# Attention and two expert layers on one core: the second layer's weight decode gets a timetable of its own, and the first layer's last output products alternate with the second layer's first input products

## The chip, the cores and the metric

One NeuronCore of a Trainium2 chip runs the whole program in one launch. The metric is the device time of one execution in microseconds (us). The engines are TensorE (PE, matmuls), VectorE (DVE), ScalarE (ACT), GpSimd (POOL) and the queue of transfers that SyncE issues (SP). Each works through its own instructions in the order of the program and waits on semaphores of the others.

## What is computed

```
q_pool = q.reshape(B, H, S // 2, 2, D).mean(axis=3)           # B 4, H 8, S 1152, D 64
attn   = softmax(q_pool @ k^T / sqrt(D))                      # per head
x      = (attn @ v) as 2304 tokens x 512

h = x @ w_in          # layer 1: 512 -> 2048
g = h * cos(h)
x = g @ w_out         # 2048 -> 512

h = x @ w_in2         # layer 2, with weights of its own
g = h * sigmoid(h)
out = g @ w_out2
```

All inputs arrive as 64-bit numbers, the weights of both layers too.

## The kernel before

**Attention, then layer 1.** The attention ends at 863 us of the span. Its matmuls are mixed with those of layer 1, which works on 9 blocks of 256 tokens (the ninth collects the left-over tokens of the four batches and can only begin after the attention). A block goes through 16 steps f. Step f makes 128 rows of h with 12 matmuls (`g1_unit`, L573): every product is made of three, of float16 high and low parts. Two steps share a PSUM buffer `h`, which ACT copies to `hk` (L589). Each 4 steps make a group G: DVE and ACT form h·cos h (DVE L601, L602, ACT sine L608, DVE L611), DVE casts the high part `gh` (L616) and POOL subtracts to get the low part `gl` (L617). The 12 matmuls of step f towards the block's output y (`g2_unit1`, L628) lag 12 steps behind. A finished y is copied by ACT (L637) to a buffer of the ring `tt` (2 buffers, the same that the cosine groups use) and stored (L640). The generator `layer1` yields after each of these units of 12 matmuls; the caller pulls it with `next(units)`.

**The decode of layer 2's weights** runs beside this. There are 16 pieces, i0 to i7 of `w_in2` and o0 to o7 of `w_out2`. A piece is loaded by SP into one of 3 buffers of the ring `wst`; ACT takes the absolute value (L220), DVE finds the maximum and shifts the bits into place (L221, L224, L229, L232), two small DVE instructions and a PE matmul (`bm`, L97) make the piece's common scale, DVE writes it (L100, L104, L108: `si` or `so`), and ACT and POOL write the float16 parts: for an i piece two ACT passes (L284, L285) and one POOL subtraction `il` (L286); for an o piece one ACT pass (L263), four POOL subtractions of 128x256 (L267), four ACT copies into the operand tables `ops` (L257) and four POOL subtractions (L258, three of 128x512 and one of 128x256). Then the ring's buffer is free, and the next piece is loaded into it.

**Layer 2** computes its h with the same `g1_unit` (its input `ys` is split by ACT L1036 and DVE L1037), and its output by outer products (`outer_steps`, L742) that use seven sums of the weight blocks instead of eight (tables `ops5`, `ops2`). The outer products need all of o0 to o7, and their tiles `op` lie in the memory that the ring `wst` gives back, so they can begin when the last o piece is done.

**What sets the order.** The generator `weight_steps` yields 4 to 5 times per piece. Before, the decode ran one piece ahead of the writing, and it was stepped once for each unit of layer 1 after the attention until the last i piece was written; then all remaining units of layer 1 ran, and the rest of the decode was stepped once for each f of layer 2. It was run to its end after block `TAIL_G - 2` of layer 2, that is after the third block. The final order of the instructions on each engine is then set by a scheduler with priorities (`ahead`, `early`).

Of the kernel before, what the change touches and what calls it, by code (L numbers as in the profile page):

```python
# [11 lines left out]
F32 = mybir.dt.float32  # L12
# [18 lines left out]
W2_BUFS, W2_PACE, W2_N = 3, 6, 1  # L31
# [15 lines left out]
def attention_moe_moe_kernel(ctx, tc, q, k, v, w_in1, w_out1, w_in2, w_out2, out):  # L47
# [32 lines left out]
    def scale_steps(m, pool, res, top, wide=False):  # L80

        n = m.shape[1]
        if wide:
            w = small.tile([128, 1], F32, name="mw", tag="mw")
            wi, mi = w.bitcast(I32), m.bitcast(I32)
            nc.vector.tensor_scalar(
                out=wi, in0=mi, scalar1=3, scalar2=0x3F800000, op0=ALU.logical_shift_left, op1=ALU.bitwise_and  # L90
            )
            nc.vector.scalar_tensor_tensor(
                out=wi, in0=mi, scalar=1 << 30, in1=wi, op0=ALU.bitwise_and, op1=ALU.bitwise_or
            )
            m = w
        bc = pool.tile([128, 2, GW], F32, tag="h", name="bm")[:, 0, 0:4]
        nc.tensor.matmul(bc[:, 0:n], mean, m, start=True, stop=True)  # L97
        yield
        s, u = res
        nc.vector.tensor_scalar(  # L100
            out=u, in0=bc[:, 0:n], scalar1=TINY, scalar2=2.0**(9 - top), op0=ALU.max, op1=ALU.mult
        )

        nc.vector.tensor_scalar(  # L104
            out=s.bitcast(I32), in0=u.bitcast(I32), scalar1=EXP_MASK, scalar2=EXP_MASK,
            op0=ALU.bitwise_and, op1=ALU.bitwise_xor,
        )
        nc.vector.tensor_scalar(  # L108
            out=u.bitcast(I32), in0=u.bitcast(I32), scalar1=EXP_MASK, scalar2=None, op0=ALU.bitwise_and
        )  # L110
# [46 lines left out]
    def weight_steps(w, srcs, stage, pspool, eng, nsub, bufs, ahead, wt_bufs=WT_BUFS):  # L157
# [16 lines left out]
        def more():  # L174
            if todo:
                kind, p, h = todo.pop(0)
                c, n = shape(kind)
                dt = I32 if wide else F32
                if w.sums and kind == "o":
                    n //= 2  # L180
                    st = stage.tile([128, 2, c, n, z], dt, tag="wst", name="wst", bufs=bufs)
                    for j in range(2):
                        o = j * (DM // 2) + p * n
                        eng.dma_start(
                            out=st[:, j].rearrange("p c f z -> p c (f z)"),
                            in_=srcs[1][:, o * z:(o + n) * z].rearrange("(c p) f -> p c f", p=128),
                        )
                    staged.append(st.rearrange("p j c f z -> p (j c) f z"))
                    return
                st = stage.tile([128, c, n, z], dt, tag="wst", name="wst", bufs=bufs)  # L190
                eng.dma_start(
                    out=st.rearrange("p c f z -> p c (f z)"),
                    in_=srcs[kind == "o"][c * 128 * h:c * 128 * (h + 1), p * n * z:(p + 1) * n * z].rearrange(
                        "(c p) f -> p c f", p=128
                    ),
                )
                staged.append(st)
# [7 lines left out]
        def decode(kind, p):  # L205
# [6 lines left out]
            for h, st in enumerate(sts):  # L212
# [5 lines left out]
                t = stage.tile([128, st.shape[1], st.shape[2]], F32, tag="wt", name="wt", bufs=wt_bufs)  # L218
# [16 lines left out]
                ts.append(st.bitcast(F32) if w.sums and kind == "o" else st.bitcast(F32)[:, :, :, 1])  # L235
# [5 lines left out]
            for _ in early(scale_steps(m1, pspool(), (s, u), 13 if w.sums and kind == "o" else 14, wide), P_CH):  # L241
                pass
# [3 lines left out]
        def halves(ops, t, p):  # L246
            o, n = ops
            f = t.shape[2]
            for x0, x1, hi, lo in w.ops:
                y0, y1 = max(o, x0), min(o + n, x1)  # L250
                if y0 >= y1:
                    continue
                h, l = (
                    x[:, y0 - x0:y1 - x0].rearrange("p o c f -> p (o c) f")[:, :, p * f:(p + 1) * f] for x in (hi, lo)
                )
                tt = t[:, (y0 - o) * (NF // 2):(y1 - o) * (NF // 2)]
                nc.scalar.activation(out=h, in_=tt, func=AF.Copy)  # L257
                nc.gpsimd.tensor_tensor(out=l, in0=tt, in1=h, op=ALU.subtract)  # L258

        def write_sums(p):  # L260
            st = decoded.pop(0)[0]
            v, f = (st[:, :, :, z] for z in (1, 0))
            nc.scalar.activation(out=v, in_=v, func=AF.Copy, scale=w.so[:, p:p + 1])  # L263
            b11, b21, b12, b22 = (v[:, i * (NF // 2):(i + 1) * (NF // 2)] for i in range(4))
            t1, t3, t2, t4 = (f[:, i * (NF // 2):(i + 1) * (NF // 2)] for i in range(4))
            for o, x, y in ((t1, b12, b11), (t3, b22, b12), (t2, b22, t1), (t4, b21, t2)):
                nc.gpsimd.tensor_tensor(out=o, in0=x, in1=y, op=ALU.subtract)  # L267
            halves((0, 2), v[:, 0:NF], p)
            yield
            halves((2, 1), b22, p)  # L270
            halves((3, 4), f, p)
            more()
            yield

        def write(kind, p):
            if w.sums and kind == "o":
                yield from write_sums(p)
                return
# [10 lines left out]
            if (kind, p) == ("i", npc - 1):  # L289
# [4 lines left out]
                nc.vector.tensor_scalar(out=w.kg, in0=w.kg, scalar1=2.0**-17 if w.sums else 2.0**-15, scalar2=None, op0=ALU.mult)  # L294
                nc.vector.tensor_scalar(out=w.ug, in0=w.ug, scalar1=2.0**14 if w.sums else 2.0**12, scalar2=None, op0=ALU.mult)
# [8 lines left out]
        r = 0 if w.sums else npc // NC  # L304
        for e in range(r):
            pp = slice(e * (128 // r), (e + 1) * (128 // r))
            nc.vector.tensor_copy(w.uoT[pp, :], w.uo.rearrange("p (c e) -> p c e", e=r)[pp, :, e])

# [460 lines left out]
    if True:  # L769
# [30 lines left out]
        def layer1():  # L800
# [6 lines left out]
            while todo or pend:  # L807
                if todo:
# [14 lines left out]
                    todo -= 1  # L823
                    yield True
# [111 lines left out]
        for n, (b, j) in enumerate(pairs):  # L936
# [13 lines left out]
            else:  # L950
# [3 lines left out]
                wgen2 = weight_steps(W2, (w_in2, w_out2), w2st, lambda: state.psw, nc.sync, 1, W2_BUFS, 1, 1)  # L954
# [108 lines left out]
        while next(units, None) is not None:  # L1063
            for _ in range(W2_N):
                if not W2.half:
                    next(wgen2, None)
# [33 lines left out]
        for n in range(NB):  # L1100
            nyb = y_load(n + 1) if n + 1 < NB else None
            gen = y_split(nyb) if nyb else None
            for f in range(NF):
                g1_unit(W2, cur, f)
                g1_evac(state.mp, W2, cur, f, False)
                next(wgen2, None)
                if gen is not None and f >= 4 and next(gen, False) is False:
                    gen = None
                if outer is None and n == TAIL_G - 1 and f == G2_AT:
                    outer = outer_steps(state.mp, opp, W2, blocks, banks, out_dst, OP_AHEAD)  # L1110
# [6 lines left out]
            if n == TAIL_G - 2:  # L1117
                run_all(wgen2)
                w2st_stack.close()
                opp = moe_stack.enter_context(tc.tile_pool(name="opp", bufs=1, reuse_waits="tile"))  # L1120
# [37 lines left out]
```

## Time and profile before

| | |
|---|---|
| median of 3 runs | 1398.57 us (1396.59 to 1401.17) |
| the profiled execution: its own time | 1398.91 us |
| span of its trace | 1396.6 us |
| PE busy | 1140.9 us (82%) |
| DVE busy | 1057.2 us (76%) |
| ACT busy | 857.6 us (61%) |
| POOL busy | 620.8 us (44%) |

All times of the trace count from the start of the span; 2.3 us of the execution's own time lie around it. An instruction is named by engine, line and the tile that it writes from the tiles that it reads. A time in brackets behind an instruction is the idle time of its engine just before it, with the instruction that ended it. Lines of the code are those of the kernel before; the same code has higher numbers in the changed kernel (L573 is L674, L628 is L729, L589 is L690, L617 is L718, L637 is L738).

### The profile page before, as it was taken

What the parts mean: (1) busy time and instruction counts of PE and PEld (TensorE: products, weight loads), DVE (VectorE), ACT (ScalarE), POOL (GpSimd) and SP (SyncE); (2) the same over time, 40 slices, a digit from 0 to 9 for tenths busy, and PEclk for the clock granted to TensorE, in tenths of its full rate; (3) what the DMA queues carried; (4) which work ended last, traced back from release to release, by engine and by line L of the source; (5) the groups of instructions that cost most, each with busy time, mean ns of one, the idle gap of its engine ahead of it and who ended that gap; (6) DMA issues with size and microseconds to landing.
All of it is one profiled execution on the core that took longest, in us unless ns stands there. A gap on an engine that the chain in (4) does not pass through costs nothing. (4 is left out here: it accounts for less than half of the span.)

```text
span 1396.6 us, 26497 instructions
## 1 busy us (share of the span) xinstructions
PE 1140.9 (82%) x10668; PEld 915.4 (66%) x10668; DVE 1057.2 (76%) x1958; ACT 857.6 (61%) x1045; POOL 620.8 (44%) x352
## 2 busy tenths in 40 slices
PE   1465356697898679898898889889996999999998
PEld 0244233375676457665666668778885888888887
DVE  7999996678778788977999995897547744444483
ACT  3687577668777688766788775553354643343352
POOL 1577266625755556645567562455556400000000
PEclk9976578799999899998999999999998999999999
DMA  7799779987799999978899965452225000000001
GB/s 234 186 237 218 195 143 209 206 161 136 159 187 180 197 206 213 184 145 194 141 210 196 224 121 113 123 120 46 59 79 106 32 23 11 29 17 16 16 31 31
DMA packets 509593, 186.26 MB, mean 133 GB/s; under 512 B 465952, under 2 KB 484384, under 8 KB 509472
## 3 DMA queue, kind: packets, MB, share of 16 engines
q1 hardware_dynamic: 509472, 184.59, 63.4%
q8 instruction: 83, 1.36, 0.4%
q14 instruction: 38, 0.31, 0.1%
HBM read 66.58 MB, written 9.44 MB: 54 GB/s over the span
## 5 line engine op out<-in xcount | busy, mean ns | idle before, releaser
L475 POOL TENSOR_TENSOR hl<-sc,hl 128x1152 f16<-128x1152 f32 x144 | 367.1, 2558 | 188.1 <-ACT hl L470 113.9
L437 PE MATMUL sp<-kT,qT 128*128 128x512 f16 (+1 forms) x768 | 193.7, 369 | 109.5 <-DVE sc L456 82.5
L456 DVE TENSOR_SCALAR_CACHE_REDUCE sc<-sp,psu 128x512 f32<-128x512 f32 (+1 forms) x288 | 229.3, 808 | 47.7 <-PE sp L437 46.3
L573 PEld LDWEIGHTS <-ih 128*128 128x128 f16 x2304 | 227.6, 100 | 39.1 <-issue 7.6
L464 ACT ACTIVATE sc<-sc,nb 128x1152 f32<-128x1152 f32 x144 | 179.9, 1250 | 93.7 <-DVE nb L461 80.9
L488 PE MATMUL pv<-vt,hlT 128*128 128x130 f16 (+1 forms) x1440 | 194.6, 237 | 41.9 <-DMA hlT<-hl 33.6
L573 PE MATMUL h<-ys,ih 128*128 128x256 f16 x1152 | 196.6, 275 | 7.0 <-DVE ys L1037 5.3
L573 PE MATMUL h<-xT,ih 128*128 128x256 f16 x1024 | 191.3, 280 | 3.8 <-ACT hk L589 2.7
L488 PEld LDWEIGHTS <-hlT 128*128 128x128 f16 (+1 forms) x1440 | 146.4, 110 | 72.1 <-DMA hlT<-hl 46.8
L437 PEld LDWEIGHTS <-qT 128*128 128x128 f16 x768 | 77.4, 109 | 174.8 <-issue 132.2
L492 PE MATMUL pv<-vt,hlT 128*128 128x65 f16 (+1 forms) x1440 | 187.1, 207 | 0.0
L470 ACT ACTIVATE hl<-sc 128x1152 f16<-128x1152 f32 x144 | 165.3, 1155 | 21.2 <-DMA xT<-xn 10.1
L628 PE MATMUL y<-gh,oh 128*128 128x256 f16 x576 | 160.1, 278 | 4.1 <-ACT y L637 4.0
L628 PE MATMUL y<-gl,oh 128*128 128x256 f16 x576 | 160.1, 278 | 2.2 <-POOL gl L617 2.2
L628 PE MATMUL y<-gh,ol 128*128 128x256 f16 x576 | 160.1, 278 | 0.0
L742 PEld LDWEIGHTS <-op 128*128 128x128 f16 x1512 | 147.9, 98 | 18.0 <-issue 0.6
L573 PE MATMUL h<-ys,il 128*128 128x256 f16 x576 | 157.9, 274 | 0.0
L492 PEld LDWEIGHTS <-hlT 128*128 128x128 f16 (+1 forms) x1440 | 142.1, 108 | 16.2 <-issue 6.5
L573 PE MATMUL h<-xT,il 128*128 128x256 f16 x512 | 143.2, 280 | 0.0
L617 POOL TENSOR_TENSOR gl<-tt,gh 128x1024 f16<-128x1024 f32 x36 | 94.0, 2612 | 97.5 <-DVE gh L616 97.5
L573 PEld LDWEIGHTS <-il 128*128 128x128 f16 x1152 | 114.5, 99 | 22.6 <-issue 7.1
L628 PEld LDWEIGHTS <-oh 128*128 128x128 f16 x1152 | 113.3, 100 | 23.1 <-issue 6.0
(296 smaller groups left out, 2038.3 us busy)
## 6 DMA issues: line engine op xcount, KB each, us to landing
wst<-in_moe_w_in_dram SPq DMA_DIRECT2D x16, 1024.0 KB, 6.2
stk<-in_k_dram SPq DMA_DIRECT2D x32, 288.0 KB, 4.2
stv<-in_v_dram SPq DMA_DIRECT2D x32, 288.0 KB, 4.5
stq<-in_q_dram SPq DMA_DIRECT2D x32, 256.0 KB, 3.1
wst<-in_moe_w_out_dram SPq DMA_DIRECT2D x8, 1024.0 KB, 6.2
wst<-in_moe_w_out_dram SPq DMA_DIRECT2D x16, 512.0 KB, 6.2
ydr<-y SPq DMA_DIRECT2D x9, 512.0 KB, 3.7
y32b<-ydr SPq DMA_DIRECT2D x9, 512.0 KB, 3.3
```

The lines of the kernel that those rows point to most:

```text
L437: nc.tensor.matmul(sp[:, o - a:o - a + n], P.qT[e][:, t, :], kT[:, o:o + n], start=(e == 0), stop=(e == 1))
L456: nc.vector.tensor_scalar(out=T.sc[:, a:z], in0=sp, scalar1=T.P.su, scalar2=None, op0=ALU.mult, op1=ALU.min, accum_out=mx[:, x:x + 1],)
L464: nc.scalar.activation(out=T.sc, in_=T.sc, func=AF.Exp, scale=-1.0, bias=nb)
L470: nc.scalar.activation(out=hi, in_=T.sc, func=AF.Copy)
L475: nc.gpsimd.tensor_tensor(out=T.hl[:, 1, :], in0=T.sc, in1=T.hl[:, 0, :], op=ALU.subtract)
L488: nc.tensor.matmul(G.pv[r, T.gi], T.hlT[:, 0, c, r], P.vt[i][:, c], start=(c == 0), stop=(c == KC - 1), skip_group_check=True,)
L492: nc.tensor.matmul(G.pv[r, T.gi, 0], T.hlT[:, 1, c, r], P.vt[i][:, c, 0], start=False, stop=(c == KC - 1), skip_group_check=True,)
L573: nc.tensor.matmul(hp, wt[:, c, f * 128:(f + 1) * 128], xt(c), start=(i == 0), stop=(i == 3 * NC - 1), skip_group_check=True,)
L617: nc.gpsimd.tensor_tensor(out=G.gl, in0=t, in1=gh, op=ALU.subtract)
L628: nc.tensor.matmul(blk.y[:, oc, :], wt[:, f, oc * 128:(oc + 1) * 128], gt[:, f % 4, :], start=(f == 0 and e == 0 and oc % 2 == 0), stop=(f ...
L742: nc.tensor.matmul(bank, t[:, e, c, :], wt[:, c, :], start=start, stop=True, skip_group_check=True)
```

## The change

The decode of layer 2 gets a function of its own, `layer2_weight_steps`, in which a piece takes 6 steps (i) or 8 (o) and each step has a tick in a table. A tick passes with each `next(wgen2)`. In `W2_TABLE` an i piece begins every 11 ticks and its steps lie 0, 2, 5, 7 and 10 ticks behind that; o0 begins at tick 88, and an o piece begins every 6 ticks with steps spread over 9 ticks. The code that made the sums in `weight_steps` goes away. After the attention a tick passes for each unit only until layer 1 has no inner (h) product left; its remaining output (y) products are then pulled one by one between the inner products of layer 2's first block. The end of the decode, the freeing of its memory and the pool of the tiles `op` move from after the third block of layer 2 into the fourth, at f = 8.

```diff
-W2_BUFS, W2_PACE, W2_N = 3, 6, 1
+W2_BUFS, W2_PACE = 3, 6
+W2_TABLE = (("i", 0, 11, (0, 2, 5, 7, 10)), ("o", 88, 6, (0, 1, 3, 4, 6, 8, 9)))
...
+            sc = scale_steps(m, pspool(), (s, u), 14 if kind == "i" else 13, True, True)
+            next(sc)
+            yield
+            next(sc)
+            yield
+            run_all(sc)
+            yield
...
+        events = []
+        for kind, at_, period, offs in table:
+            for p in range(npc):
+                if (kind, p) == ("i", 0):
+                    events.append((at_ + offs[4], 0, first))
+                    continue
+                g = []
+                for k, o in enumerate(offs):
+                    events.append((at_ + p * period + o, len(events), (kind, p, g)))
+        events.sort(key=lambda x: x[:2])
+        now = 0
+        for when, _, what in events:
+            while now < when:
+                now += 1
+                yield
...
                     pend.append((cur, f))
                     todo -= 1
+                    state.todo = todo
                     yield True
...
-        while next(units, None) is not None:
-            for _ in range(W2_N):
-                if not W2.half:
-                    next(wgen2, None)
+        while state.todo:
+            next(units)
+            next(wgen2)
         while not W2.half:
             next(wgen2)
...
                 next(wgen2, None)
+                next(units, None)
...
                 if outer is None and n == TAIL_G - 1 and f == G2_AT:
+                    run_all(wgen2)
+                    w2st_stack.close()
+                    opp = moe_stack.enter_context(tc.tile_pool(name="opp", bufs=1, reuse_waits="tile"))
                     outer = outer_steps(state.mp, opp, W2, blocks, banks, out_dst, OP_AHEAD)
...
-            if n == TAIL_G - 2:
-                run_all(wgen2)
-                w2st_stack.close()
-                opp = moe_stack.enter_context(tc.tile_pool(name="opp", bufs=1, reuse_waits="tile"))
```

How the instructions move is seen on three engines. Below, groups of the tail are counted G0, G1, ... from the first whose y unit follows the attention; G8 to G11 are the four groups of the ninth block.

ACT before, around the copies of group G7 (`hk_11398`); `wst_10932` is piece o1 and `wst_10859` is o0:

```order
L589 ACTIVATE hk_11285<-h_11299,ca_10346 128x512
L220 ACTIVATE wt_11037<-wst_10932 128x1024
L608 ACTIVATE tt_11339<-tt_11339,halfpi_73 128x1024
L263 ACTIVATE wst_10859<-wst_10859,so2_114 128x1024
L589 ACTIVATE hk_11398<-h_11360,ca_10346 128x512
L637 ACTIVATE y32_11354<-y_10880,cy_10337 128x256 x4
```

ACT now, around the copies of the same group (`hk_11321`); `wst_10728` is piece i4 and `wst_11253` is i7:

```order
L335 ACTIVATE ih2_10392<-wst_10728,si2_112 128x4x256
L690 ACTIVATE hk_11190<-h_11151,ca_10346 128x512
L336 ACTIVATE wst_10728<-wst_10728,si2_112 128x1024
L690 ACTIVATE hk_11190<-h_11207,ca_10346 128x512
L306 ACTIVATE wt_11613<-wst_11253 128x1024
L709 ACTIVATE tt_11247<-tt_11247,halfpi_73 128x1024
L690 ACTIVATE hk_11321<-h_11278,ca_10346 128x512
L738 ACTIVATE y32_11267<-y_10789,cy_10337 128x256 x4
```

Ahead of the same copy stands now the absolute value of i7, a piece that is loaded into the buffer that i4 gives free.

POOL before, where the last groups of layer 1 meet the o pieces (`gl_11671` is G9, `gl_11785` G10, `gl_11898` G11; `wst_10932` is o1):

```order
L617 TENSOR_TENSOR gl_11671<-tt_11672,gh_11670 128x1024
L258 TENSOR_TENSOR ops2_12072<-wst_10859,ops2_12072 128x16x32
L267 TENSOR_TENSOR wst_10932<-wst_10932 128x256 x2
L258 TENSOR_TENSOR ops5_10394<-wst_10932,ops5_10394 128x16x32
L267 TENSOR_TENSOR wst_10932<-wst_10932 128x256
L258 TENSOR_TENSOR ops5_10394<-wst_10932,ops5_10394 128x8x32
L258 TENSOR_TENSOR ops5_10394<-wst_10932,ops5_10394 128x16x32
L267 TENSOR_TENSOR wst_10932<-wst_10932 128x256
L617 TENSOR_TENSOR gl_11785<-tt_11786,gh_11784 128x1024
```

POOL now (`gl_11631` is G9, `gl_11755` G10; `wst_11431` is o0, `wst_11597` is o1):

```order
L718 TENSOR_TENSOR gl_11631<-tt_11632,gh_11630 128x1024
L353 TENSOR_TENSOR wst_11431<-wst_11431 128x256 x4
L367 TENSOR_TENSOR ops5_10394<-wst_11431,ops5_10394 128x16x32
L367 TENSOR_TENSOR ops5_10394<-wst_11431,ops5_10394 128x8x32
L367 TENSOR_TENSOR ops5_10394<-wst_11431,ops5_10394 128x16x32
L353 TENSOR_TENSOR wst_11597<-wst_11597 128x256 x2
L367 TENSOR_TENSOR ops2_11915<-wst_11431,ops2_11915 128x16x32
L367 TENSOR_TENSOR ops5_10394<-wst_11597,ops5_10394 128x16x32
L353 TENSOR_TENSOR wst_11597<-wst_11597 128x256
L367 TENSOR_TENSOR ops5_10394<-wst_11597,ops5_10394 128x8x32
L367 TENSOR_TENSOR ops5_10394<-wst_11597,ops5_10394 128x16x32
L718 TENSOR_TENSOR gl_11755<-tt_11756,gh_11754 128x1024
```

Before, o0 stood ahead of G6 but for its last subtraction, and eight instructions stood between G9 and G10; now all eight of o0 and six of o1 stand between G9 and G10.

DVE now, at the scale of piece o2 (`bm_12195`); `wt_12427` belongs to piece o4, which is loaded into the buffer of o1:

```order
L1139 SCALAR_TENSOR_TENSOR ys_12143<-y32b_11921,ys_12071,ys_12143 128x1024
L307 TENSOR_SCALAR wt_12427,wm_12426<-wt_12427 128x1024
L103 TENSOR_SCALAR uo2_115<-bm_12195 128x1
L310 TENSOR_SCALAR wt_12427<-wt_12427 128x1024
L107 TENSOR_SCALAR so2_114<-uo2_115 128x1
L315 SCALAR_TENSOR_TENSOR wst_12192<-wst_12192,wt_12427 128x1024
```

DVE before, at the scale of o2 (`bm_12213`):

```order
L1037 SCALAR_TENSOR_TENSOR ys_12221<-y32b_12078,ys_12178,ys_12221 128x1024
L100 TENSOR_SCALAR uo2_115<-bm_12213 128x1
L89 TENSOR_SCALAR mw_12415<-wm_12375 128x1
L104 TENSOR_SCALAR so2_114<-uo2_115 128x1
L92 SCALAR_TENSOR_TENSOR mw_12415<-wm_12375,mw_12415 128x1
```

The scale of o2 stands now behind two instructions of o4's decode; before, only small instructions stood there. On PE the units of 12 keep their kinds and number; between matmuls 1028 and 1371 after the attention the last y units, which ran as one row of 145 matmuls, alternate 12 by 12 with inner products, and the first outer product stands behind 1851 matmuls where it stood behind 1779.

## Rows read from the trace of the kernel before

**Rows 1.** Windows: length, busy PE, PEld, DVE, ACT, POOL, clock, DMA share, GB/s

```profile
863.30:955.00 91.70, 78.48 (x668) 67.34 (x669) 81.27 (x121) 52.33 (x61) 42.14 (x18) 0.94 0.48 117
955.00:1059.10 104.10, 100.91 (x924) 89.85 (x922) 53.74 (x73) 44.52 (x63) 58.90 (x44) 1.00 0.27 65
1059.10:1099.80 40.70, 28.47 (x234) 23.73 (x232) 29.96 (x49) 21.76 (x30) 28.27 (x24) 0.83 0.28 59
1099.80:1383.00 283.20, 283.20 (x2597) 253.66 (x2595) 157.80 (x227) 119.01 (x167) 0.00 (x0) 1.00 0.06 22
```

**Rows 2.** Waits of PE from 863 to 1100: us in total, times, longest

```profile
PE bm L97 <- DVE mw L92: 15.8, 5, 6.2
PE h L573 <- DVE ys L1037: 5.3, 1, 5.3
PE y L628 <- ACT y L637: 3.3, 1, 3.3
```

**Rows 3.** Timeline of PE: start, duration, instruction

```profile
863.49 0.27 PE L628 MATMUL y<-gh,oh 128*128 128x256 f16 x1
...
898.63 0.37 PE L628 MATMUL y<-gh,oh 128*128 128x256 f16 x1 [3.32 <-ACT y L637]
...
955.04 0.27 PE L628 MATMUL y<-gh,oh 128*128 128x256 f16 x1
...
1059.13 0.37 PE L97 MATMUL bm<-mw,mean 128*128 128x1 f32 x2
...
1099.64 0.38 PE L742 MATMUL oy<-ops,op 128*128 128x256 f16 x2
```

**Rows 4.** The chain that ended last: start, duration, 12 matmuls

```profile
964.37 1.31 PE y L628 x12
```

**Rows 5.** Windows: the stretch behind the wait at 898.63, columns as in rows 1

```profile
898.63:901.96 3.33, 3.33 (x17) 2.31 (x17) 3.33 (x7) 3.33 (x5) 0.00 (x0) 0.51 1.12 189
```

**Rows 6.** Timeline of DVE and POOL, single instructions

```profile
908.60 2.14 POOL L617 TENSOR_TENSOR gl<-tt,gh 128x1024 f16<-128x1024 f32 x1 [2.13 <-DVE gh L616]
...
908.80 3.03 DVE L229 SCALAR_TENSOR_TENSOR wst<-wst,wt 128x1024 int32<-128x1024 int32 x1
...
929.83 1.23 DVE L229 SCALAR_TENSOR_TENSOR wst<-wst,wt 128x1024 int32<-128x1024 int32 x1
...
969.06 0.69 DVE L616 CAST gh<-tt 128x1024 f16<-128x1024 f32 x1
```

**Rows 7.** Timeline of POOL at the o pieces

```profile
951.21 6.84 POOL L267 TENSOR_TENSOR wst<-wst 128x256 f32<-128x256 f32 x4 [0.51 <-ACT wst L263]
...
1032.53 2.46 POOL L267 TENSOR_TENSOR wst<-wst 128x256 f32<-128x256 f32 x3 [17.36 <-ACT wst L263]
1034.95 2.91 POOL L258 TENSOR_TENSOR ops<-wst,ops 128x512 f16<-128x512 f32 x3
...
1096.47 1.15 POOL L258 TENSOR_TENSOR ops<-wst,ops 128x512 f16<-128x512 f32 x1 [0.77 <-ACT ops L257]
```

**Rows 8.** Timeline of ACT, and of DVE, around 1062

```profile
1061.88 1.12 ACT L220 ACTIVATE wt<-wst 128x1024 f32<-128x1024 f32 x1 [1.86 <-DMA wst<-in_moe_w_out_dram]
1062.89 1.21 ACT L263 ACTIVATE wst<-wst,so 128x1024 f32<-128x1024 f32 x1
...
1060.35 0.15 DVE L104 TENSOR_SCALAR so<-uo 128x1 int32<-128x1 int32 x1
```

**Rows 9.** Groups, 863.3 to 1099.8: busy, mean ns, idle before and releasers

```profile
L589 ACT ACTIVATE hk<-h,ca 128x512 f32<-128x512 f32 x24 | 16.4, 682 | 20.9 <-PE h L573 20.9
L284 ACT ACTIVATE ih<-wst,si 128x1024 f16<-128x1024 f32 x8 | 9.8, 1241 | 7.4 <-DVE si L104 7.2
L221 DVE TENSOR_SCALAR_CACHE_REDUCE wt<-wt 128x1024 f32<-128x1024 f32 x13 | 15.7, 1211 | 18.9 <-ACT wt L220 18.9
L220 ACT ACTIVATE wt<-wst 128x1024 f32<-128x1024 f32 x13 | 15.0, 1154 | 24.1 <-DMA wst<-in_moe_w_out_dram 13.9 <-DVE wst L229 7.5 <-DMA wst<-in_moe_w_in_dram 2.6
```

**Rows 10.** DMA issues, 860 to 1100: count, KB each, median us to landing

```profile
wst<-in_moe_w_out_dram SPq DMA_DIRECT2D x16, 512.0 KB, 6.2
wst<-in_moe_w_in_dram SPq DMA_DIRECT2D x5, 1024.0 KB, 5.5
```

More of the change, by code (lines that the diff above doesn't have):

```diff
@@ L77, in attention_moe_moe_kernel, with scale_steps @@
     GW = 256
-    def scale_steps(m, pool, res, top, wide=False):
+    def scale_steps(m, pool, res, top, wide=False, apart=False):
         n = m.shape[1]
@@ L95, in scale_steps @@
             m = w
+            if apart:
+                yield
         bc = pool.tile([128, 2, GW], F32, tag="h", name="bm")[:, 0, 0:4]
@@ L177, in more @@
                 c, n = shape(kind)
[L178 to L190, printed above, removed]
+                st = stage.tile([128, c, n, z], I32 if wide else F32, tag="wst", name="wst", bufs=bufs)
                 eng.dma_start(
@@ L217, in decode @@
                     continue
-                t = stage.tile([128, st.shape[1], st.shape[2]], F32, tag="wt", name="wt", bufs=wt_bufs)
+                t = stage.tile([128, c, n], F32, tag="wt", name="wt", bufs=wt_bufs)
                 ti = t.bitcast(I32)
@@ L234, in decode @@
                 )
-                ts.append(st.bitcast(F32) if w.sums and kind == "o" else st.bitcast(F32)[:, :, :, 1])
+                ts.append(st.bitcast(F32)[:, :, :, 1])
                 yield
@@ L240, in decode @@
                 nc.vector.tensor_reduce(out=m1, in_=m, axis=AX.X, op=ALU.max)
-            for _ in early(scale_steps(m1, pspool(), (s, u), 13 if w.sums and kind == "o" else 14, wide), P_CH):
+            for _ in early(scale_steps(m1, pspool(), (s, u), 14, wide), P_CH):
                 pass
@@ L244, in decode @@
             yield
[L246 to L273, printed above, removed]
         def write(kind, p):
-            if w.sums and kind == "o":
-                yield from write_sums(p)
-                return
             c, n = shape(kind)
@@ L293, in write @@
                 nc.vector.tensor_reduce(out=w.ug, in_=w.ui, axis=AX.X, op=ALU.max)
-                nc.vector.tensor_scalar(out=w.kg, in0=w.kg, scalar1=2.0**-17 if w.sums else 2.0**-15, scalar2=None, op0=ALU.mult)
-                nc.vector.tensor_scalar(out=w.ug, in0=w.ug, scalar1=2.0**14 if w.sums else 2.0**12, scalar2=None, op0=ALU.mult)
+                nc.vector.tensor_scalar(out=w.kg, in0=w.kg, scalar1=2.0**-15, scalar2=None, op0=ALU.mult)
+                nc.vector.tensor_scalar(out=w.ug, in0=w.ug, scalar1=2.0**12, scalar2=None, op0=ALU.mult)
         for i in range(ahead):
@@ L302, in weight_steps @@
             yield from write(*x)
-        r = 0 if w.sums else npc // NC
+        r = npc // NC
         for e in range(r):
@@ L953, in attention_moe_moe_kernel @@
                 w2st = w2st_stack.enter_context(tc.tile_pool(name="w2st", bufs=1, reuse_waits="tile"))
-                wgen2 = weight_steps(W2, (w_in2, w_out2), w2st, lambda: state.psw, nc.sync, 1, W2_BUFS, 1, 1)
+                wgen2 = layer2_weight_steps(W2, (w_in2, w_out2), w2st, lambda: state.psw, nc.sync, W2_BUFS, W2_TABLE)
                 bg.append(slowly(islice(wgen2, 4), W2_PACE))
```

110 lines of the change are left out of this document (added).

## The prediction, made before the changed kernel had run

> **What bounds the kernel now.** I read the windows first. Up to 863 us the order of the instructions on every engine is the same before and after, so the attention is no part of the sum. [...] The question is how early the outer products can start, because from that point on PE only runs, and the end moves with them.
>
> To compare points in a program whose order changes I use a lag of PE. At full clock 12 matmuls take 1.31 us [rows 4], 0.1092 each. The lag is the time since 863.49, where the first y matmul behind the attention starts, less 0.1092 times the matmuls since then. I counted those in the order of the program. Before, it reads [rows 3]:
>
> - matmul 267, at 898.63: 35.14 − 29.16 = 6.0
> - matmul 651, at 955.04: 91.55 − 71.1 = 20.4
> - matmul 1563, at 1059.13: 195.64 − 170.7 = 25.0
> - matmul 1779, the first outer product, at 1099.64: 236.15 − 194.3 = 41.9
>
> So 41.9 us are lost in all, of which 20.4 by 955, 4.6 in the middle and 16.9 at the end. The waits of PE say to whom: 15.8 us to five scales `mw` of the decode, 5.3 to a `ys`, 3.3 to a copy of y [rows 2]. [...]
>
> Next come DVE and POOL. The shift L229 takes 1.23 us alone and 3.03 us when POOL's `gl` runs at 908.60 to 910.74 [rows 6]: it stands until POOL is through. I therefore take DVE's operations with two tensor inputs (1.23) and its copies and casts (0.69), and all of POOL's, as one line of work, the pair. By the windows the two are busy 81.3 and 42.1 us in 91.7 us [rows 1], in which the waits for each other are counted as busy.
>
> [...]
>
> **The change, part by part.** No operation is added or removed, and the DMAs are the same 21 loads, so every term is a change of place.
>
> *A1, the first y copy.* One `il` less (2.1 us, as `gl` [rows 6], equal in size) stands in POOL ahead of the `gl` that y's buffer waits for. The wait of 3.32 at matmul 267 shrinks to about 1.2, and y starts at 896.5: lag 4.0 instead of 6.0.
>
> *A2, the ring of staging buffers.* From there the i pieces pace each other, because i5 needs i2's buffer and i7 needs i4's. From 896.4: six ACT passes (the copy of y among them) 5.0, `il` of i2 2.1, load 5.5 to 6.2 [rows 10], absolute value 1.15, four or five DVE operations (1.2, and 0.69 each) 4.5, `gl` 2.1, ten DVE operations 10.5, then scale, sine, `ih`, a copy and the second pass (1.15, 1.24, 0.68, 1.24 [rows 9]) 4.3, `il` of i4 2.1, load 5.5 to 6.2. The absolute value of i7 thus ends at about 941, and the ACT row in the section on the change puts the first copy of G7 behind it and a sine: 942.5 to 943.2. PE needs that copy at matmul 627, where it arrives at 863.49 + 68.5 + 5 = 937. It waits 5.5 to 6, and half clock costs 2 more. Lag at 651: about 13, against 20.4. The five scale waits of before mostly go, since the scales now stand 100 and more matmuls apart.
>
> *B, the alternation.* y of G8 (matmul 1035) needs the buffer of a y copy, which needs `gl` G9 at 991.2 by the same walk. PE arrives at 989.3 and loses about 3.5 with the copy, and 1.7 of half clock: lag 18. Behind `gl` G9 POOL now has 14 subtractions of o0 and o1 ahead of `gl` G10. An o piece takes POOL 4 × 0.82 + 2.91 + 1.15 = 7.3 [rows 7], so these are 12.7 us, and about 7 of DVE go between: `gl` G10 ends near 1013. PE wants it at matmul 1179, 863.49 + 128.7 + 18 = 1010. It waits 3: lag 21 to 22. These waits cost nothing in the end, for the pair is later than PE:
>
> *C, the o stage.* From 991.2 POOL has eight o pieces (58) and two `gl` (4.3) to do, 62.3. DVE has six decodes of 3.15 (0.69 + 2 × 1.23), the rest of two cosine groups 5.8, two `ys` 2.5 and four sums for the operands 4.9, together 32. In line that is 94.3: not before 1085.5. To this comes time in which POOL stands: about 6 at o2, whose scale now stands behind the decode of o4 on DVE, which waits for the load of o4 into o1's buffer; 2 at o3, whose `bm` sits behind matmul 1383. DVE uses some 1.5 of it. POOL's last subtraction ends at about 1092. Before, the first outer product started 2.0 behind POOL's last (1096.47 + 1.15 to 1099.64 [rows 7, 3]). So it starts at 1094.0, with 1851 matmuls done: lag 130.5 + 100.0 − 202.1 = 28.4.
>
> *Sum.* 41.9 − 28.4 = 13.5 us less. Taken from the profiled execution, 1398.91 − 13.5 = 1385.4; that execution is 0.3 above the median of 1398.57, so I give 1385. The moved end of the decode and the new pool cost nothing of their own: the last o piece is due then anyway. Behind the first outer product no wait is added, since DVE and ACT are 56% and 42% busy there and POOL idle [rows 1].
>
> **A rule against it.** ACT works in order: `so` was ready at 1060.50, but the pass L263 stood behind an absolute value that waited 1.86 us for its DMA, and started at 1062.89 [rows 8]. In the new order three more passes that PE waits for stand behind such an absolute value. That costs the 5.5 to 6 of A2, and is in the sum. [...]
>
> **Rivals.**
>
> *The pair is never idle* (gain 20). If o2's scale and o3's `bm` come in time, POOL ends at 1085.5 and the first outer product starts at 1087.5: lag 21.9, 1379. For it: my walk is long, and the loads land in 5.5 to 6.2 [rows 10] where I took the later. Against it: the DVE rows stand as they stand. Where DVE and POOL overlap a little more than I count, some 4 us go as well: 1375.
>
> *No change* (within 4). POOL stood 17.36 us at 1032.53 for L263, though the work was there [rows 7]. If such an idle time comes back, 9 to 17 us more than I count, the outer products start as late as before: 1395 to 1402. For it: the o stage again hangs on three buffers. Against it: a tick passes now with each unit, and the decode of an o piece begins while two others are open.
>
> *Slower.* The place is the ring in the o stage. If the scale of each o piece stands behind the decode of the piece two later, as o2's does, then POOL waits in each turn for a load 6.2, an absolute value 1.15, the maximum 1.21 and the scale 0.15 [rows 8 to 10], 8.7 in all. My floor of 1087.5 lies 20 us before the break-even (1107.5, the start with matmul 1851 at the lag of before). So two such turns still gain 2 to 3, and from three on it is slower. With four the outer products start at 1122: 1398.9 + 14.9 = 1414; with three 1405. For it: o2's row; the 6.84 us that POOL took for four subtractions at 951.21 against 2.46 for three [rows 7] say that the pair can take longer than I count. Against it: from o3 on the order puts the scale of a piece ahead of the maximum of the piece two later.
>
> *The change does nothing to the o stage* is covered by the second rival.
>
> **How the numbers follow.** My forecast, a gain of 6 to 20 (1379 to 1393), gets 0.58; the idle-free pair, 1375 to 1379, 0.16; no change, 1395 to 1402, 0.14; slower, 1404 and more, 0.12. This kernel's measurement can tell 0.3%, 4.2 us, from no change; so faster is 0.58 + 0.16 = 0.74, same 0.14, slower 0.12. The range runs from 1375 to 1398: it takes in the first two cases and the lower half of the third.
>
> **What would show it.** In the profile of the changed kernel: the five waits of `bm` for `mw` are down to a few us; one wait of PE for the copy `hk` L690 of 5 to 7 us near 937 to 943, and a small one for `gl` L718 near 1010; POOL nearly without idle from 991 to 1092, with one gap of about 6 at o2; the first outer product at 1094; then 283 us of unbroken PE. [...]

## The result, and the profile after

The changed kernel took 1384.93 us (median of 4 runs, 1384.42 to 1388.85) against 1399.87 us before; ratio 0.9899, 95% interval 0.9867 to 0.9931. The forecast was 1385, a gain of 13.5 us; the profiled executions stand at 1384.48 and 1398.91, 14.4 apart.

The windows of the changed kernel in the stages of [rows 1] (length, busy PE, PEld, DVE, ACT, POOL, granted clock, DMA share, GB/s), with the last cut at the new start of the outer products:

```profile
863.30:955.00 91.70, 86.53 (x781) 76.62 (x779) 67.62 (x97) 45.08 (x53) 39.09 (x14) 0.98 0.36 96
955.00:1059.10 104.10, 94.66 (x828) 82.32 (x826) 70.61 (x106) 53.64 (x75) 67.21 (x50) 0.95 0.41 89
1059.10:1093.40 34.30, 32.55 (x298) 28.62 (x296) 23.27 (x44) 21.44 (x29) 22.92 (x22) 1.00 0.28 72
1093.40:1369.00 275.60, 275.60 (x2527) 246.73 (x2525) 156.57 (x222) 116.21 (x163) 0.00 (x0) 1.00 0.06 20
```

PE does 781 matmuls in the first stage, where it did 668; in the second it does fewer, at 0.95 of the clock; from 1093.4 on it is busy without a break, as it was from 1099.8 on before. The waits of PE from 862 to 1100, to be laid beside [rows 2]:

```profile
PE y L729 <- ACT y L738: 6.4, 2, 3.3
PE h L674 <- ACT gs L690: 4.3, 3, 2.6
PE h L674 <- ACT hk L690: 1.9, 1, 1.9
PE bm L100 <- DVE ym L116: 1.4, 1, 1.4
PE bm L100 <- DVE uo L103: 1.3, 1, 1.3
PE y L729 <- POOL gl L718: 0.8, 1, 0.8
```

With one of 0.2 they sum to 16.3 us. Before it was 24.4 in the three rows of [rows 2] and 4.1 in smaller ones, 28.5. The 15.8 us of waiting for the scale `mw` and the 5.3 for `ys` are gone. Where the remaining ones stand, in PE's timeline (brackets: idle time and who ended it), with the first y matmul behind the attention and the first outer product as the ends:

```profile
864.10 0.27 PE L729 MATMUL y<-gh,oh 128*128 128x256 f16 x1
...
897.44 0.37 PE L729 MATMUL y<-gh,oh 128*128 128x256 f16 x1 [3.03 <-ACT y L738]
...
940.46 0.38 PE L674 MATMUL h<-xrT,ih 128*128 128x256 f16 x2 [1.94 <-ACT hk L690]
...
990.64 0.37 PE L729 MATMUL y<-gh,oh 128*128 128x256 f16 x1 [3.35 <-ACT y L738]
...
1009.88 0.27 PE L729 MATMUL y<-gl,oh 128*128 128x256 f16 x1 [0.75 <-POOL gl L718]
...
1043.58 0.58 PE L674 MATMUL h<-ys,ih 128*128 128x256 f16 x2 [2.61 <-ACT gs L690]
...
1082.69 0.38 PE L674 MATMUL h<-ys,ih 128*128 128x256 f16 x2 [1.44 <-ACT gs L690]
...
1093.48 0.38 PE L843 MATMUL oy<-ops,op 128*128 128x256 f16 x2
```

The lag (time since the first y matmul, less 0.1092 us for each matmul since) is 229.38 − 202.1 = 27.3 at the first outer product, 41.9 before. That product has no wait of its own in the last row: PE came to it after its operands were there. The count of matmuls leaves out the two short ones of each scale (38 before, 40 now).

**A split that all readings below use.** Up to the first y matmul every kernel here does the same work, but for one scale that falls just before or just behind it; on PE, other than the prediction says, some twenty matmuls between 817 and 834 us stand in another order before and after the change. Yet that matmul stands between 859.8 and 870.7 us in the traces. The rest of the span is steadier: it is 533.1 us before (1396.6 − 863.49) and 518.5 after (1382.6 − 864.10). Take the lag at the first outer product off, and 491.2 is left in both. So a time is the attention's end, plus 491.2, plus the lag. For each kernel, "rest" is the span less the start of the first y matmul, and the lag is the rest less 491.2; taken from the first outer product itself, rest and lag differ by 490.9 to 491.8, and by 492.5 with o0 at tick 104, where PE still waits behind that product.

| kernel | first y | rest | lag | ratio of times to the kernel before |
|---|---|---|---|---|
| before | 863.49 | 533.1 | 41.9 | |
| changed | 864.10 | 518.5 | 27.3 | 0.9899 (0.9867 to 0.9931) |
| changed, second trace | 868.36 | 520.4 | 29.2 | 0.9904 (0.9877 to 0.9932) |
| timetable only | 859.83 | 524.4 | 33.2 | 0.9901 (0.9871 to 0.9932) |
| alternation only | 869.47 | 528.0 | 36.8 | 0.9961 (0.9940 to 0.9982) |
| without 24 sums | 867.74 | 520.1 | 28.9 | 0.9884 (0.9854 to 0.9915) |
| with 24 sums twice | 868.35 | 528.6 | 37.4 | 0.9968 (0.9946 to 0.9990) |
| o decode's first steps later | 862.57 | 524.0 | 32.8 | 0.9958 (0.9933 to 0.9984) |
| o0 at tick 96 | 863.69 | 525.2 | 34.0 | 0.9946 (0.9925 to 0.9967) |
| o0 at tick 104, every 5 | 862.06 | 526.3 | 35.1 | 0.9965 (0.9940 to 0.9991) |
| o0 at tick 94, every 5 | 862.09 | 527.5 | 36.3 | 0.9950 (0.9928 to 0.9972) |
| i pieces every 10 ticks | 870.65 | 513.1 | 21.9 | 0.9828 (0.9791 to 0.9866) |
| the same, second trace | 868.92 | 513.1 | 21.9 | 0.9843 (0.9814 to 0.9873) |
| i pieces every 8 ticks | 866.03 | 517.2 | 26.0 | 0.9870 (0.9846 to 0.9893) |

### The profile page after: what moved, and what is told of

Same layout as the page of the kernel before. It is cut to its first block, busy times and chain, and to the rows that moved or that the text cites. A ratio compares the mean times of both kernels' runs of the same rounds, so it can differ in the third digit from the quotient of the medians.

```text
span 1382.6 us, 26493 instructions
## 1 busy us (share of the span) xinstructions
PE 1142.2 (83%) x10668; PEld 916.0 (66%) x10668; DVE 1063.5 (77%) x1958; ACT 856.3 (62%) x1045; POOL 619.7 (45%) x352
## 5 line engine op out<-in xcount | busy, mean ns | idle before, releaser
L557 DVE TENSOR_SCALAR_CACHE_REDUCE sc<-sp,psu 128x512 f32<-128x512 f32 (+1 forms) x288 | 229.4, 808 | 41.9 <-PE sp L538 40.3
L589 PEld LDWEIGHTS <-hlT 128*128 128x128 f16 (+1 forms) x1440 | 148.1, 111 | 70.0 <-DMA hlT<-hl 45.4
L674 PE MATMUL h<-xT,ih 128*128 128x256 f16 x1024 | 186.6, 276 | 3.9 <-ACT hk L690 3.3
L593 PEld LDWEIGHTS <-hlT 128*128 128x128 f16 (+1 forms) x1440 | 143.6, 108 | 15.6 <-issue 6.4
```

What stands on the lines that cost most here:

```text
L557: nc.vector.tensor_scalar(out=T.sc[:, a:z], in0=sp, scalar1=T.P.su, scalar2=None, op0=ALU.mult, op1=ALU.min, accum_out=mx[:, x:x + 1],)
L589: nc.tensor.matmul(G.pv[r, T.gi], T.hlT[:, 0, c, r], P.vt[i][:, c], start=(c == 0), stop=(c == KC - 1), skip_group_check=True,)
L593: nc.tensor.matmul(G.pv[r, T.gi, 0], T.hlT[:, 1, c, r], P.vt[i][:, c, 0], start=False, stop=(c == KC - 1), skip_group_check=True,)
L674: nc.tensor.matmul(hp, wt[:, c, f * 128:(f + 1) * 128], xt(c), start=(i == 0), stop=(i == 3 * NC - 1), skip_group_check=True,)
```

## The experiments

Two theories stood at the start. **The pair**, from step C of the prediction: the common work of DVE and POOL decides when the outer products can start, and the end follows. **The queue**: PE reaches the outer products without waiting for them, and the time is the sum of PE's single waits, most of which come through ACT's row, where a pass waits behind the one ahead of it (1062.89 behind 1061.88 in [rows 8]).

**The timetable without the alternation**, and **the alternation without the timetable.**

```diff
-        while state.todo:
-            next(units)
-            next(wgen2)
+        while next(units, None) is not None:
+            if not W2.half:
+                next(wgen2)
...
-                next(units, None)
```

> The new timetable without the alternation: all units of layer 1 run before layer 2's first inner product, as before the change. Theory 1 (the pair): the common work of DVE and POOL sets when the outer products start. The scale of o1 now stands behind 1323 matmuls instead of 1035, about 31 us of PE later, and POOL stands idle between o0 and o1; the outer products start at 1102 to 1107, behind 1935 matmuls, and the time is 1386 to 1391. Theory 2 (the queue): PE never waits for the outer operands, the time is the sum of single waits that reach PE through ACT's row of copies; the waits for y's copy (3.35 us) and for gl (0.75 us) in the alternating stretch go, so 1380 to 1385. A rival to both, that the alternation is the whole gain: 1397 or more.

The second is the kernel before with these lines:

```diff
+                    state.todo = todo
...
+        while state.todo:
+            next(units)
+            if not W2.half:
+                next(wgen2, None)
...
+                next(units, None)
```

> The old decode with its old steps, and only the alternation added. By my prediction's terms the first part (lag 20.4 by 955 us) stays as before the change and only the o stage can gain: 1391 to 1395 by both theories. If the alternation is the whole gain: 1385. If the timetable is the whole gain: 1398.

PE's waits (line, releaser: us in total, times, longest), first with the timetable only, then with the alternation only:

```profile
PE y L729 <- ACT y L738: 7.0, 2, 4.0
PE h L674 <- ACT gs L690: 6.9, 5, 3.4
PE y L729 <- POOL gl L718: 2.8, 1, 2.8
```

```profile
PE bm L97 <- DVE mw L92: 11.8, 6, 3.4
PE h L573 <- ACT gs L589: 7.6, 5, 3.0
```

The timetable takes 8.7 us off the lag by itself, and no wait for `mw` is left with it; the alternation takes 5.1 and leaves 11.8 us of them. Together that is 13.8 of the 14.6. By the whole times the timetable alone gains as much as the whole change (0.9901 against 0.9899 and 0.9904), so what the alternation adds to it, 4 to 6 us of lag, is read from single traces and not seen in the times. The timetable alone came out at 1387.01, inside the pair theory's 1386 to 1391. Its first outer product stands at 1103.84 (forecast 1102 to 1107), but its trace begins early: counted from the first y matmul that is 244.0, where the forecast meant 238 to 243. The y waits that the queue theory wanted gone are still there. With the alternation alone (1394.33) the stretch from matmul 1011 to 1213 added 0.3 us of lag, and 15 came behind it. Each part does some of it, as both theories had it; neither is decided.

**Less work for POOL, and more.** In the first the plain blocks stand in for the sums of pieces o2 to o7.

```diff
+            if p < 2:
                 for o, x, y in ((t1, b12, b11), (t3, b22, b12), (t2, b22, t1), (t4, b21, t2)):
...
-            halves(3, 4, f)
+            halves(3, 4, f if p < 2 else v)
```

> The changed kernel, without the four subtractions of 128x256 for pieces o2 to o7; the plain blocks stand in for the sums, so the result is not the reference's. This takes 24 x 0.82 = 19.7 us from POOL in the o stage. Theory 1 (the pair): the outer products start as much earlier as POOL gets through, 10 to 17 us, and the time falls to 1368 to 1375. Theory 2 (the queue): PE reached the first outer product without a wait, so only the waits for the copies gs behind POOL's turn go, with their half clock: 1379 to 1385.

```diff
-                nc.gpsimd.tensor_tensor(out=o, in0=x, in1=y, op=ALU.subtract)
+                for _ in range(2 if p > 1 else 1):
+                    nc.gpsimd.tensor_tensor(out=o, in0=x, in1=y, op=ALU.subtract)
```

> The changed kernel with the four subtractions of 128x256 issued twice for pieces o2 to o7 (the second writes the same values), 19.7 us more for POOL in the o stage. Leaving these 19.7 us out changed the lag by +1.9 only. Pair theory: POOL's end sets the first outer product, so its time moves 15 to 20 us out, and the lag, with the first outer product behind 1947 matmuls instead of 1851, is 32 to 37. Queue theory: POOL has idle time of 20 us between 1013 and 1073, most of the doubling fits there and the scheduler has put 96 more matmuls ahead of the outer products: lag 27 to 31.

POOL's last subtraction and PE's first outer product, without the sums:

```profile
1082.84 4.04 POOL L368 TENSOR_TENSOR ops<-wst,ops 128x512 f16<-128x512 f32 x4 [1.77 <-ACT ops L367]
...
1088.52 0.38 PE L844 MATMUL oy<-ops,op 128*128 128x256 f16 x2
```

Counted from the first y matmul (867.74), POOL ends at 219.1, 8.3 us earlier than in the changed kernel (1091.48 − 864.10 = 227.4), and the first outer product starts 8.6 earlier. But it now stands behind 1755 matmuls instead of 1851, 10.5 us of PE's work less, so the lag is not smaller: 28.9. Fewer inner products stand ahead, and PE does them later. The pair theory's 1368 to 1375 is out; the queue theory's 1379 to 1385 is missed by 1.4 at the median (1386.39). With the sums doubled the lag is 37.4, just above the 32 to 37 of the pair theory and out of the queue theory's 27 to 31. There PE's longest late wait is for a split on DVE, which the pair counts in one line with POOL's work:

```profile
1097.14 0.37 PE L675 MATMUL h<-ys,ih 128*128 128x256 f16 x1 [3.25 <-DVE ys L1140]
```

So POOL's work stands at a limit: more of it cost, less of it gave nothing, since PE's waits are made elsewhere.

**The place of the absolute values in ACT's row.** In the changed kernel the wait of 2.61 us at 1043.58 is made here (ACT, the absolute value of o5 and the copy `gs` behind it):

```profile
1041.83 1.12 ACT L306 ACTIVATE wt<-wst 128x1024 f32<-128x1024 f32 x1 [2.51 <-DMA wst<-in_moe_w_out_dram]
1042.86 0.67 ACT L690 ACTIVATE gs<-h,ca 128x512 f32<-128x512 f32 x1
```

```diff
-    ("o", 88, 6, (0, 1, 3, 4, 6, 8, 9))
+    ("o", 88, 6, (2, 3, 5, 6, 7, 8, 9))
```

> The changed kernel with the first four steps of an o piece two to three ticks later in the table, so that the absolute values of o5 and later stand behind more copies gs in ACT's row. Theory 2 (the queue): the wait of 2.61 us for gs behind the absolute value of o5, which waited 2.51 us for its load, shrinks or goes, with half clock 2 to 4 us less: 1381 to 1383. Theory 1 (the pair): the o pieces come later, so POOL ends later: 1385 to 1390.

Two of PE's waits for `gs` with that table:

```profile
1043.59 0.38 PE L674 MATMUL h<-ys,ih 128*128 128x256 f16 x2 [0.76 <-ACT gs L690]
...
1073.91 0.58 PE L674 MATMUL h<-ys,ih 128*128 128x256 f16 x2 [2.83 <-ACT gs L690]
```

The wait at that place went, as the queue theory had it, and one of 0.76 us came 24 matmuls later: between matmuls 1419 and 1467 the lag grows by 1.0 us with it, instead of 4.6. The whole lag is 3.6 to 5.5 larger all the same, and the time above both forecasts (median 1396.11; the traced execution took 1388.58), since from there on five waits for `gs` of 0.8 us and more followed, up to 2.83, and POOL ended 2.1 later. The theory names the carrier of this wait rightly and not the price of a table.

**Later o pieces.** The o entry of the table was changed to `("o", 96, 6, ...)`, `("o", 104, 5, ...)` and `("o", 94, 5, ...)`.

> The changed kernel with o0 starting at tick 96 instead of 88. In POOL's row only o0 stands ahead of gl G10 and G11, and o1 stands behind G11. What the first runs leave as theory (the queue): the time is the attention's end plus 491.2 us plus PE's lag, and the lag is the sum of PE's single waits; the alternating stretch (matmuls 1035 to 1251), which added 9 us of lag in the changed kernel and 0.4 in the kernel with the old decode, adds 4 to 6, the rest about as much as before (8.6): lag at the first outer product 22 to 26, against 27.3. The pair theory: POOL's work begins 8 us later, so the outer products start later and the lag is 30 to 35.

> o0 at tick 104, an o piece every 5 ticks: in POOL's row all of the o pieces stand behind gl G11, and the first outer product stands behind more than 1995 matmuls. Queue theory: the alternating stretch adds under 2 us of lag; the rest is open, since the decode ends later, in layer 2's fourth block and beyond: lag 18 to 26. Pair theory: POOL begins the o pieces some 20 us later than in the changed kernel; the lag is 40 or more.

> o0 at tick 94 and a piece every 5 ticks instead of 6. Queue theory: as with o0 at 96 in the alternating stretch (4 to 6 us of lag); the scales stand earlier in PE's row (o2 to o5 at 1347, 1395, 1503, 1570), so PE may wait for them; lag 22 to 30. Pair theory: as the changed kernel or up to 5 us later, 27 to 32, since POOL gets the same pieces a little later.

With o0 at 96, PE's longest sum of waits; and PE's first outer product with o0 at 104:

```profile
PE y L729 <- ACT y L738: 8.2, 2, 5.1
```

```profile
1116.31 0.39 PE L843 MATMUL oy<-ops,op 128*128 128x256 f16 x2 [1.95 <-ACT op L785]
```

All three were worse than the changed kernel, by 5 to 9 us of rest against its two traces. In the alternating stretch (from the last scale before 1035 to 1191 or 1218) they still added 7 to 9.5 us of lag: the wait for y's copy is 5.0 to 5.1, although o1, or all o pieces, stood behind the last `gl` in POOL's row. In the changed kernel it is 3.35, but there 1.33 for a scale stands just ahead of it, so the place costs nearly the same. The queue theory as I had it, that the o pieces ahead of `gl` make this wait, falls; its lags of 22 to 26, 18 to 26 and 22 to 30 were measured as 34.0, 35.1 and 36.3. Of the pair theory, 30 to 35 for tick 96 holds; 40 and more for tick 104 and 27 to 32 for 94 do not. With tick 104 PE does wait at the first outer product: there the operands came later than PE.

**Earlier i pieces.** What is late at y's copy may then be G9's own `gl`, and ahead of it the last `il`. So the i entry was changed from `("i", 0, 11, ...)` to `("i", 0, 10, ...)`, and to 8.

> The changed kernel with an i piece every 10 ticks instead of 11; the o table stays. In POOL's row the last il stands two groups earlier, before G7's gl and not between G8 and G9, and the scales of i4 to i7 stand 36 to 144 matmuls earlier in PE's row. Queue theory: the lag up to matmul 900 stays at 8 to 10, DVE and POOL are freer when G9 is due, so the wait of 3.35 us for y's copy at matmul 1035 shrinks to about 1 and its half clock goes: lag at the first outer product 22 to 25 against 27.3. If the scales come too early in PE's row, PE waits for them (as in the kernel before) and the lag at 900 is 12 or more. Pair theory: the same common work, lag 26 to 28.

> An i piece every 8 ticks: all of the il stand ahead of G8. The same question further out: 36 to 150 matmuls of PE fewer between the scales. If the room between the scales is what removed PE's waits for them (15.8 us before), some of these return: lag at matmul 627 10 to 16 against 8, and the whole no better than 27. If not, lag 20 to 25.

PE's waits with 10 ticks, all of 0.1 us and more:

```profile
PE h L674 <- ACT gs L690: 6.7, 7, 1.8
PE h L674 <- ACT hk L690: 2.7, 1, 2.7
PE y L729 <- ACT y L738: 2.3, 1, 2.3
PE bm L100 <- DVE ym L116: 1.9, 1, 1.9
```

And the first with 8 ticks:

```profile
PE h L674 <- ACT hk L690: 8.2, 5, 3.7
```

With 10 ticks the second wait for y's copy is gone, and with it the granted 0.50 behind it (the clock reads 1.00 from 962 to 1066): G9's `gl` ends 119.05 us behind the first y matmul (986.71 + 2.99 − 870.65) instead of 124.68, and the lag grows by 2.8 from matmul 987 to 1231, where it grew by 10.4 from 987 to 1215. The end is 21.9, just under the queue theory's 22 to 25. With 8 ticks the decode crowds the groups of the middle stretch: PE waits five times for `hk`, the lag at matmul 627 is 13.7 (8.0 with 10 ticks; the forecast said 10 to 16 if the scales come too early), and the whole lands at 26.0, where that forecast said no better than 27. It was `hk` and not `mw` that was waited for.

**The split tried, and the better table beside the changed kernel.**

> The changed kernel as it is, a second time. All readings of the experiments so far rest on one trace of each kernel, split at the first y matmul behind the attention. If that split is sound, the part behind it is the same to within 1 us (518.5 in the first trace) and only the attention's end moves, which lay between 859.8 and 870.7 us in the traces so far. If the split is not sound, the part behind it scatters by several us too, and the differences of 2 to 5 us between the tables mean nothing.

> The kernel with an i piece every 10 ticks, a second time and on the same chip as the changed kernel: the part behind the attention 513.1 again to within 1 us if the split is sound, and the median 4 to 6 us under that of the changed kernel in this call.

The rest came out at 520.4 (first 518.5) and 513.1 (first 513.1). So the split is good to about 2 us, not to 1: differences of 2 us between tables mean nothing, the 5 to 7 us between 10 and 11 ticks do. Side by side the medians were 1379.69 and 1386.47 us, 6.8 apart (forecast 4 to 6), and no execution of the one took as long as any of the other: the table with 10 ticks beats both kernels.

## Why the prediction was right, and where its steps were not

**A1, the first y copy: the copy as forecast, the wait not.** I forecast a lag of 4.0 at matmul 267; it is 33.34 − 29.16 = 4.2. The `gl` that the copy needs, before and now, with the copy itself:

```profile
891.83 4.11 POOL L617 TENSOR_TENSOR gl<-tt,gh 128x1024 f16<-128x1024 f32 x1 [6.75 <-DVE gh L616]
```

```profile
890.64 4.11 POOL L718 TENSOR_TENSOR gl<-tt,gh 128x1024 f16<-128x1024 f32 x1 [6.76 <-DVE gh L717]
...
894.79 0.84 ACT L738 ACTIVATE y<-y,cy 128x256 f32<-128x256 f32 x2 [3.79 <-POOL gl L718]
```

Counted from the first y matmul, `gl` starts at 26.5 and not at 28.3, 1.8 us earlier (forecast 2.1): before, POOL ran three `il` in a row ahead of it (7.92 us), now two (5.90). But the wait for y's copy is 3.03, not 1.2, since PE comes 1.5 us earlier too: the wait for a scale ahead of it went, and the lag where this wait begins is 1.2 instead of 2.7. ACT itself stood free for 3.79 us here until `gl` came, so it is DVE and POOL that make this wait.

**A2, the ring: the place right, the size too large.** ACT's row at the first copy of G7 is as the order had it:

```profile
937.66 1.13 ACT L306 ACTIVATE wt<-wst 128x1024 f32<-128x1024 f32 x1 [5.10 <-DMA wst<-in_moe_w_in_dram]
938.70 1.13 ACT L709 ACTIVATE tt<-tt,halfpi 128x1024 f32<-128x1024 f32 x1
939.74 0.67 ACT L690 ACTIVATE hk<-h,ca 128x512 f32<-128x512 f32 x1
```

The copy ended at 940.4, not 943, after a walk of some 45 us; PE came at 938.5, not 937. So the term "waits 5.5 to 6, and half clock costs 2 more" measured 1.94 and nothing in this trace, 2.67 and 1.9 in the second trace. Lag at matmul 771: 7.9 and 10.6, where I had about 13 at 651. The five waits for the scale's `mw` went, as forecast.

**B, the alternation: near.** The wait at y of G8 is 3.35 (forecast 3.5) and the granted clock behind it 0.50, as the windows of the changed kernel behind 990.6 and, for contrast, behind 940.4 show:

```profile
990.60:995.00 4.40, 4.36 (x21) 3.04 (x21) 1.90 (x3) 4.37 (x7) 4.32 (x6) 0.50 0.30 121
```

```profile
940.40:944.00 3.60, 3.54 (x33) 3.18 (x33) 3.60 (x8) 2.78 (x7) 0.00 (x0) 1.00 0.36 143
```

The 2 us of half clock in A2 and the 1.7 in B were my estimate from the one stretch of [rows 5], 3.33 us at 0.51. No run shows that such a stretch follows every wait: behind 940.46 the clock read 1.00, while the 4.40 us at 0.50 behind 990.6 cost about 2.2.

`gl` G10 ended at 1009.83 (forecast 1013) and cost 0.75 instead of 3. Not foreseen were 1.3 and 1.4 us for scales on DVE. Lag at matmul 1215: 18.5, and 20.4 in the second trace, against 21 to 22. That the o pieces in POOL's row make this stretch dear was wrong (ticks 96 and 104). The second y copy begins at 989.04, 0.26 us behind the end of G9's `gl`, so this wait too is set by DVE and POOL: with 10 ticks that `gl` came 5.6 us earlier and the wait was gone.

**C, the o stage: the end right, its role wrong.** POOL in the changed kernel:

```profile
985.80 2.98 POOL L718 TENSOR_TENSOR gl<-tt,gh 128x1024 f16<-128x1024 f32 x1 [4.42 <-DVE gh L717]
...
1024.88 3.43 POOL L353 TENSOR_TENSOR wst<-wst 128x256 f32<-128x256 f32 x3 [9.77 <-ACT wst L349]
...
1035.98 4.40 POOL L353 TENSOR_TENSOR wst<-wst 128x256 f32<-128x256 f32 x3 [2.10 <-ACT wst L349]
...
1073.27 2.64 POOL L353 TENSOR_TENSOR wst<-wst 128x256 f32<-128x256 f32 x2 [7.88 <-ACT wst L349]
...
1090.32 1.16 POOL L367 TENSOR_TENSOR ops<-wst,ops 128x512 f16<-128x512 f32 x1 [0.78 <-ACT ops L366]
```

From the end of G9's `gl` (988.78) to POOL's last end (1091.48) are 102.7 us, where I had 94.3 of common work and about 6.5 idle (988.78 + 100.8 = 1089.6; I wrote 1092 from a later `gl`). The gap at o2 is there, 9.77 long with 6.4 us of DVE's part of the pair in it (two maskings, three shifts and a split by their durations alone); the one at o3 is 2.10 (forecast 2), and one of 7.88 at o6 is not in the sum. Which of DVE's operations stand in one line with POOL was my estimate from the two shifts of [rows 6]. In the changed kernel nine of the twelve casts L717 took 0.68 or 0.69 us and three, beside POOL's subtractions, 2.50 to 2.63 (2.63 at 1007.75, with `gl` at 1007.71); the maximum L307 took 1.21 or 1.22 beside them too (1.22 at 993.10). The two-input operation L703 took 1.22 at 891.55, and there it was `gl` that took 4.11 against 2.13 at 1012.98.

The reason that I gave for o2's gap, o4's load, was not it:

```profile
1019.43 0.28 PE L100 MATMUL bm<-mw,mean 128*128 128x1 f32 x2
...
1020.30 1.13 ACT L306 ACTIVATE wt<-wst 128x1024 f32<-128x1024 f32 x1
...
1023.34 0.15 DVE L107 TENSOR_SCALAR so<-uo 128x1 int32<-128x1 int32 x1
```

The absolute value of o4 (1020.30) waited for no transfer. The scale's matmul stands late in PE's row, at 1019.43, 18 us behind the `mw` that it reads (1000.49 to 1001.60), and DVE's row takes 3.9 us more until `so`. The gap at o6 is of the kind of the rival "slower", a whole turn of the ring. The load of o6 began when POOL gave o3's buffer free, its absolute value had to wait for it, and the scale took until 1071.87:

```profile
1052.49 1.61 SPq L293 DMA_DIRECT2D wst<-in_moe_w_out_dram  x2
...
1060.16 1.17 ACT L306 ACTIVATE wt<-wst 128x1024 f32<-128x1024 f32 x1 [0.51 <-DMA wst<-in_moe_w_out_dram]
```

The first outer product stands at 1093.48, forecast 1094.0. But the sentence "the pair is later than PE", and with it that these waits of PE "cost nothing in the end", failed: PE did not wait for the operands, and 19.7 us less for POOL gave nothing. The first outer product's place in PE's row follows POOL's work: it stands behind 1755, 1851 and 1947 matmuls without the sums, with them and with them twice. I take it that the scheduler chose it so; that it starts 2 us behind POOL's end shows no cause. POOL's end is a bound all the same: with the alternation alone and with o0 at tick 104 PE did wait at this product, 0.59 and 1.95 us, and started it 1.24 us behind POOL's end in both. The changed kernel's 2.00 leaves 0.8 us to that.

What set the time is the sum of PE's waits, 28.5 us before and 16.3 after, and the clock: by the windows, 0.06 × 91.7 + 0.17 × 40.7 = 12.4 us were lost to it before, and 0.02 × 91.7 + 0.05 × 104.1 = 7.0 after. A part of this fell where PE stood anyway, and must not count twice. Two waits before, and two now (columns as in [rows 1], the clock third from the end):

```profile
1062.27:1068.44 6.17, 0.01 (x1) 0.00 (x0) 5.41 (x10) 6.12 (x8) 4.26 (x4) 0.78 0.62 99
1069.49:1074.79 5.30, 0.00 (x1) 0.00 (x0) 5.30 (x6) 0.66 (x1) 4.53 (x4) 0.50 0.00 0
```

```profile
894.41:897.44 3.03, 0.00 (x1) 0.00 (x0) 1.76 (x4) 2.65 (x6) 0.34 (x1) 0.90 0.01 3
987.29:990.64 3.35, 0.00 (x1) 0.00 (x0) 2.17 (x4) 3.35 (x7) 2.91 (x3) 0.75 0.04 7
```

That is 0.22 × 6.17 + 0.50 × 5.30 = 4.0 us before and 0.10 × 3.03 + 0.25 × 3.35 = 1.1 now. Without it the clock cost 8.4 and 5.9, and waits and clock make 12.2 + 2.5 = 14.7 us of less loss, against 14.6 measured. So of the 17.5 us of lag before that the three rows of [rows 2] leave (41.9 − 24.4), 8.4 are clock, 4.1 smaller waits, and 5.0 neither, of which the short matmuls of the scales, left out of the count, are a part. That remainder is 5.1 now.

So the size came out right in part by luck: the sum took the lag from the pair's end, near which the first outer product stands whatever PE waits for, and the lags of A2 and B, some 5 and 3 us too large, did not enter it. ACT's order, which I weighed against the change, carries 4.5 of the 16.3 us of waits that are left, the 1.94 and the 2.61: the rows at 937.66 to 939.74 and at 1041.83 and 1042.86 show it, and the table that moved the second absolute value removed that wait. Of the rivals, the idle-free pair (1379) and no change (1395 to 1402) did not come. Nor did the slower one, which needed three turns of the ring: the gap at o2 has another cause, and only o6's is such a turn.

Open is why tables that shift the o pieces by a few ticks cost 5 to 9 us: each changes several waits at once, and no run here changed one alone.

## What to carry to other kernels

Where one engine runs without a break from some point on, count its lag against its own full speed at several points of its row: the difference of two kernels then splits into places, and parts that only scatter (here the attention's end, by 11 us) drop out. When waits and a low clock are added up, a low clock inside a wait counts once. A start that stands right behind its operands in a scheduled program is no proof that the operands set it; leave some of their work out and look whether the lag falls. The pace of a decode beside other work has a best value: earlier pieces are out of the way of the groups behind them, up to the point where they crowd the copies that the matmuls wait for. Here 11, 10 and 8 ticks gave lags of 27 to 29, 22 and 26.

## What the runs showed that was not expected

The same work up to the attention's end took between 859.8 and 870.7 us in 14 traces, a scatter larger than most effects tried here. And waits at one place were followed by different clocks in two traces of the same kernel. With 10 ticks the first wait for y's copy took 2.35 us in one trace and 2.33 in the other; in the 4 us behind it the granted clock was 0.62 in the one and 1.00 in the other. In the changed kernel the wait for `hk` at matmul 627 differed in length too: behind 1.94 us PE went on at a granted 1.00, behind 2.67 us the window of the second trace reads 0.73, 1.9 us more lag:

```profile
945.00:949.00 4.00, 3.21 (x20) 2.49 (x20) 4.00 (x10) 3.18 (x8) 0.00 (x0) 0.73 0.25 97
```
